# A fused transformer block on one core: the linear-attention factor products by k in two halves, and three fp32 row sums as pairs of rounded matmuls

## The chip, the core and the metric

The kernel runs on one core of one Trainium2 chip. The metric is the device time of one execution in microseconds. Before the change it is 561.61 us, the median of 3 runs (560.68 to 561.68).

## What is computed

The reference, cut to what matters here (S = 2048 tokens, D = 512, 32 heads of 16):

```python
mod = silu(c) @ w_mod                       # six vectors: sa, ca, ga, sb, cb, gb
h = layernorm(x) * (1 + ca) + sa
q, k, v = split(h @ wqkv)                   # 32 heads of 16
phi = lambda t: where(t > 0, t + 1, exp(t)) + 1e-6
kv  = einsum("bhsd,bhse->bhde", phi(k), v)
z   = sum over s of phi(k)
o   = (phi(q) @ kv) / (phi(q) . z + 1e-6)
x = x + ga * (o @ wo)
h = layernorm(x) * (1 + cb) + sb
x = x + gb * (((h @ w_gate) * (h @ w_up)) @ w_down)
```

All tensors are fp32.

## The kernel before

**Number format.** A fp32 operand is held as a pair of tiles: a high part, rounded to the matmul's rounded fp32 format by a ScalarE copy, and a low part, the difference, taken by VectorE. `split` (L192) makes such a pair, `split_raw` (L196) with fresh buffers, and `product` (L202) multiplies two lists of pairs with three matmuls a pair: high by high (L206), high by low (L207), low by high (L208). A plain fp32 matmul needs no pair.

**Stages.** Tokens come in 16 tiles of 128 (4 chunks of 4). The first stage makes the k side: for each tile the normalized rows times the k weights, phi, and `t_tile` (L350), which accumulates x-hat transposed times phi(k) in four PSUM banks `tacc`. So v is never formed for each token: at the end `tacc` is scaled by ca and gets zb x sa added, which gives four factors of 128 rows (k = 0 to 3, L736 to L743), and these times the v weights give kv. Beside it, `z_add` (L336) sums phi(k) over the tiles in `zacc`. The main loop (L612) runs over tiles 4 to 15. In each iteration i the matmuls of a later projection stand first, then the elementwise work, then `t_tile(i)`, then what the table `extra` (L552) holds for i: splits of the v weights (4 to 7), the modulation sums `mod_part` of further vectors (8 to 14), the split of the wo weights (14), and the row sums.

**Row sums.** `mod_row` (L184) sums a 128 x 512 tile over its partitions and spreads the result to all partitions with one fp32 matmul by a 128 x 128 tile of ones (L186). It does so for ga (i = 11) and gb (i = 15). The same is done for `zacc` in the last iteration (L654), whose result `zb` (L656) everything in the next stage needs.

**The stage between.** L731 to L771 is an order written out by hand. `den_z`, `den_p`, `den_r`, `den_a`, `den_b` make the denominators: `den_p` (L676) is phi(q) times zb, on GpSimd unless `on` names VectorE; `den_r` (L682) the sum over each head; `den_b` (L691, L692) adds a constant and takes the reciprocal for a chunk; `den_c` (L711) multiplies phi(q) by it. `q_a` and `q_b` (L310, L311 on ScalarE; L314 on VectorE) make phi(q) from a projection's bank, and `q_b` frees that bank. The four factors are scaled on ScalarE (L738), completed on VectorE (L739), split (L193, L194), and multiplied with the v weights in 48 matmuls of 128 columns (L749), group g of 128 columns by group, with all k inside. The block-diagonal mask (L757) and a split give `kvp`; `w_out` (L719) multiplies it with the wo pairs, scales by ga (L725) and splits the result to `wp`. q projections 6 to 10 stand between these. Then tile by tile `turn_a` (four transposes of phi(q), L782), `turn_h` and `turn_l` (the split, L786 and L790) and `y_a` (12 matmuls with `wp`, L807) make the attention output; the second half of the kernel, from there on, is the gated block.

**What sets the order.** The program's order is each engine's order: nothing is rescheduled. Buffers come from pools: 99 SBUF tiles (`tiles`), and 4 + 4 PSUM banks (`ps_acc`, `ps_w`). `bank()` takes from `ps_w`, so a projection waits until the bank that it gets has been read.

Of the kernel before, what the change touches and what calls it, by code (L numbers as in the profile page):

```python
# [14 lines left out]
P = 128  # L15
# [7 lines left out]
def tile_adaln_block(  # L23
# [57 lines left out]
    def bank():  # L81
        return T(ps_w, "bank")
# [1 line left out]

    ident = consts.tile([P, P], F32, name="ident")
    make_identity(nc, ident)
    ones = consts.tile([P, P], F32, name="ones")
    nc.gpsimd.memset(ones, 1.0)
    mask = consts.tile([P, P], F32, name="mask")
    nc.gpsimd.memset(mask, 1.0)  # L90
    m3 = mask.rearrange("p (b i) -> p b i", i=DH)
# [67 lines left out]
    def silu():  # L159
        nc.scalar.activation(ce, ct, AF.Exp, scale=-1.0)  # L160
        nc.vector.tensor_scalar(ce, ce, 1.0, None, op0=ALU.add)
        nc.vector.reciprocal(ce, ce)
        nc.vector.tensor_mul(sc, ct, ce)
# [9 lines left out]
    def mod_col(acc, ps):  # L173

        for b in range(KD):
            nc.tensor.matmul(ps[:, b:b + 1], acc[:, b * P:(b + 1) * P], ones[:, 0:1], start=True, stop=True)
        return ps

    def col_out(v, ps, add):
# [1 line left out]
        nc.vector.tensor_scalar(t, ps[:, :KD], add, None, op0=ALU.add)  # L181
        return t

    def mod_row(v, acc):  # L184
        ps = bank()
        nc.tensor.matmul(ps, ones, acc, start=True, stop=True)  # L186
        t = consts.tile([P, D], F32, name=f"row{v}")
        nc.scalar.activation(t, ps, AF.Copy)
        return t
# [9 lines left out]
        split(raw, h[:raw.shape[0]], l[:raw.shape[0]], low)  # L199
        return h, l  # L200

    def product(ps, pairs):  # L202

        n = len(pairs)
        for i, ((ah, al), (bh, bl)) in enumerate(pairs):
            nc.tensor.matmul(ps, ah, bh, start=i == 0, stop=False)  # L206
            nc.tensor.matmul(ps, ah, bl, start=False, stop=False)  # L207
            nc.tensor.matmul(ps, al, bh, start=False, stop=i == n - 1)  # L208

    def product2(pss, pairs):  # L210

# [152 lines left out]
    def q_b(i):  # L364
        phi_b(q_ps.pop(i), phq[i])
# [16 lines left out]
    def sums_in(b):  # L382
        return ps_idle if b == 1 else ps_m
# [12 lines left out]

    def block_one(v, b):
        at = at_of(v, b)
        nc.tensor.matmul(sums_in(b)[:, at:at + 1], sums[v, b // 2][:, b % 2 * P:(b % 2 + 1) * P], ones[:, 0:1],
                         start=True, stop=True)  # L400

    def block_out(b):
# [38 lines left out]

    keep_on(18)
    n0.stats(0)
    silu()
    n0.stats(1)
    n0.rstd_of(0, 2)
# [97 lines left out]
    def mod_load(*vs):  # L544
        raw_m.update({v: load_mod(v) for v in vs})

    def mod_part(v, *ks):
        if 0 in ks:
            accs[v] = B("f")
        mod_acc(accs[v], raw_m[v], ks)  # L550
# [4 lines left out]
             7: lambda: (wv.extend(split_raw(r) for r in raw_v[3:4]),),  # L555
             8: lambda: (mod_part(2, 0, 1), mod_load(3)),
             9: lambda: (mod_part(2, 2, 3), mod_load(4)),
             10: lambda: (mod_part(3, 0, 1, 2), mod_load(5)),
             11: lambda: (mod_part(3, 3), mod_part(4, 0, 1), rows.update({2: mod_row(2, accs[2])})),
             12: lambda: (raw_o.extend(load(wo_v[k], "raw") for k in range(KD)), mod_part(4, 2, 3), cols.update({3: col_out(3, mod_col(accs[3], bank()), 0.0)})),  # L560
             13: lambda: (mod_part(5, 0, 1, 2), cols.update({4: col_out(4, mod_col(accs[4], bank()), 1.0)})),
             14: lambda: (mod_part(5, 3), wo_s.extend(split_raw(x) for x in raw_o)), 15: lambda: rows.update({5: mod_row(5, accs[5])})}
    q_at = {4: 3}
    ahead = {}

# [46 lines left out]
    for i in range(4, NT):  # L612
# [31 lines left out]
            q_b(q_at[i])  # L644
        if i + 1 < NT:
            z_add(i + 1)
        if ch + 2 < NCH and j == 2:
            nx2.nmr_of()
            nx2.xhat(0, 1)
        if ch + 2 < NCH and j == 3:  # L650
            nx.xhat(3)
        if i == NT - 1:
            zps = bank()
            nc.tensor.matmul(zps, ones, zacc, start=True, stop=True)  # L654
# [78 lines left out]
    den_a(0, 0, 1, on=nc.vector)  # L733
    ps = proj(6, wq)
    fs, tt = [], []
    for k in range(KD):  # L736
        f = B("n")
        nc.scalar.activation(f, tacc[k], AF.Copy, scale=ca[:, k:k + 1])  # L738
        nc.vector.scalar_tensor_tensor(f, zb, sa[:, k:k + 1], f, op0=ALU.mult, op1=ALU.add)  # L739
# [536 lines left out]
```

## Time and profile before

| | |
|---|---|
| median of 3 runs | 561.61 us |
| profiled execution | 561.47 us |
| span in its profile | 559.8 us |
| TensorE clock granted | 1.00 |
| TensorE busy, matmuls | 551.9 us, 2544 instructions |
| VectorE busy | 379.8 us, 648 instructions |
| ScalarE busy | 294.2 us, 531 instructions |
| GpSimd busy | 207.4 us, 226 instructions |

The profile calls TensorE PE (its weight loads PEld), VectorE DVE, ScalarE ACT, GpSimd POOL, and the DMA-issuing engine SP. A row of a timeline gives the start and the duration in microseconds, the engine, the source line, the operation, output and input tiles by name, the shape, and how many instructions were merged; in brackets stands the idle time before it and what ended it. Matmul durations are modelled and overlap, so that consecutive starts tell more than durations.

### The profile page before, as it was taken

How to read it: one execution, taken by the hardware profiler on the slowest of the kernel's cores; microseconds unless marked ns; L12 is line 12 of the kernel's file. 1: busy time of each engine (PE TensorE's matmuls, PEld its weight loads, DVE VectorE, ACT ScalarE, POOL GpSimd, SP SyncE). 2: the span in 40 equal slices, each digit the busy share in tenths (PEclk: the TensorE clock that was granted, in tenths of full speed). 3: DMA queues.
4: the chain of work that ended last, by engine and by line, in shares of the span. 5: the costliest groups of instructions: out<-in, count | busy, mean ns of one | idle time of the engine just before them, and what ended most of it. 6: DMA issues, size and time to landing. Idle time of an engine off the chain costs nothing.

```text
span 559.8 us, 7391 instructions
## 1 busy us (share of the span) xinstructions
PE 551.9 (99%) x2544; PEld 453.5 (81%) x2544; DVE 379.8 (68%) x648; ACT 294.2 (53%) x531; POOL 207.4 (37%) x226
## 2 busy tenths in 40 slices
PE   7999999999999999999999999999999999999997
PEld 5888888888888888888888888878888888888775
DVE  5968779869898998865655766862455545444653
ACT  3876858446476877663545355553444334334420
POOL 2000000003327646343556644485424455554200
PEclk9999999999999999999999999999999999999999
DMA  8910224202230020151446136598353211200004
GB/s 254 384 39 1 75 76 150 77 0 71 80 114 2 0 76 0 39 159 68 150 151 195 32 122 221 178 363 286 114 157 87 57 39 48 71 0 1 0 1 150
DMA packets 50133, 57.24 MB, mean 102 GB/s; under 512 B 6384, under 2 KB 28912, under 8 KB 50096
## 3 DMA queue, kind: packets, MB, share of 16 engines
q1 hardware_dynamic: 50096, 56.77, 31.8%
q8 instruction: 20, 0.33, 0.3%
q14 instruction: 17, 0.14, 0.1%
HBM read 43.12 MB, written 13.63 MB: 101 GB/s over the span
## 4 chain that ended last, share of the span: by engine, by line
PE 94%; DVE 3%; DMA 1%; SPq 0%; issue 0%; ACT 0%; POOL 0%
PE bank L970 38%; PE acc L807 8%; PE acc L1048 7%; PE acc L1049 7%; PE acc L1050 7%; PE bank L206 5%; PE bank L207 5%; PE bank L208 5%; PE acc L357 2%; PE acc L355 2%; PE acc L356 2%; PE bank L271 2%; PE acc L439 1%; DMA x<-in_A_x_dram 1%; PE bank L782 1%; PE acc L271 1%
## 5 line engine op out<-in xcount | busy, mean ns | idle before, releaser
L970 PE MATMUL bank<-h,w 128*128 128x512 f32 (+1 forms) x924 | 215.8, 390 | 0.0
L970 PEld LDWEIGHTS bank<-h,w 128*128 128x128 f32 (+1 forms) x924 | 170.8, 185 | 38.6 <-issue 0.4
L976 ACT ACTIVATE bank<-bank 128x512 f32<-128x512 f32 (+1 forms) x44 | 25.6, 581 | 151.2 <-PE bank L970 151.1
L956 POOL TENSOR_TENSOR w<-raw,w 128x256 fp32r<-128x256 f32 (+3 forms) x44 | 46.1, 1048 | 157.2 <-ACT w L949 150.0
L996 DVE TENSOR_TENSOR phi<-bank,g 128x512 f32<-128x512 f32 (+1 forms) x22 | 15.1, 688 | 83.5 <-PE bank L970 79.8
L1048 PE MATMUL acc<-w,kh 128*128 128x512 f32 (+1 forms) x176 | 68.6, 390 | 0.0
L1049 PE MATMUL acc<-w,kh 128*128 128x512 f32 (+1 forms) x176 | 68.6, 390 | 0.0
L1050 PE MATMUL acc<-w,kl 128*128 128x512 f32 (+1 forms) x176 | 68.5, 389 | 0.0
L956 POOL TENSOR_TENSOR w<-t,w 128x512 fp32r<-128x512 f32 (+1 forms) x44 | 57.4, 1305 | 0.0
L1055 DVE TENSOR_TENSOR x<-acc,x 128x512 f32<-128x512 f32 x80 | 50.3, 681 | 8.6 <-PE acc L1050 8.6
L206 PE MATMUL bank<-w,h 128*128 128x512 f32 x112 | 44.8, 400 | 0.0
L208 PE MATMUL bank<-w,h 128*128 128x512 f32 x112 | 43.7, 390 | 0.0
L207 PE MATMUL bank<-w,h 128*128 128x512 f32 x112 | 43.6, 390 | 0.0
L676 POOL TENSOR_TENSOR f<-h,zb 128x512 f32<-128x512 f32 x12 | 17.1, 1439 | 67.8 <-ACT zb L656 49.2
L249 POOL TENSOR_TENSOR rstd<-ve,half 128x4 f32<-128x4 f32 (+3 forms) x12 | 11.2, 930 | 83.0 <-DVE ve L246 71.4
L807 PE MATMUL acc<-w,xh 128*128 128x512 f32 x128 | 40.7, 399 | 0.0
L1048 PEld LDWEIGHTS acc<-w,kh 128*128 128x128 f32 (+1 forms) x176 | 33.0, 188 | 7.1
L1050 PEld LDWEIGHTS acc<-w,kl 128*128 128x128 f32 (+1 forms) x176 | 33.0, 188 | 7.0
L1049 PEld LDWEIGHTS acc<-w,kh 128*128 128x128 f32 (+1 forms) x176 | 33.1, 188 | 6.9
L938 POOL TENSOR_TENSOR t<-raw,t 128x256 f32<-128x256 f32 (+1 forms) x44 | 36.9, 838 | 1.7
L1022 DVE TENSOR_TENSOR g<-bank,u 128x512 f32<-128x512 f32 (+1 forms) x22 | 15.2, 691 | 27.0 <-ACT u L976 27.0
L264 ACT ACTIVATE n<-x,nmr,rstd 128x512 f32<-128x512 f32 x31 | 23.7, 808 | 14.6 <-DVE nmr L254 14.4
(159 smaller groups left out, 1011.3 us busy)
## 6 DMA issues: line engine op xcount, KB each, us to landing
x<-in_A_x_dram SPq DMA_DIRECT2D x24, 256.0 KB, 5.2
raw<-in_w_mod_dram SPq DMA_DIRECT2D x24, 256.0 KB, 3.8
raw<-in_B_w_gate_dram SPq DMA_DIRECT2D x40, 128.0 KB, 3.0
raw<-in_B_w_up_dram SPq DMA_DIRECT2D x40, 128.0 KB, 3.1
raw<-in_B_w_down_dram SPq DMA_DIRECT2D x20, 256.0 KB, 3.1
side_s<-h SPq DMA_DIRECT2D x16, 256.0 KB, 2.5
h<-side_s SPq DMA_DIRECT2D x16, 256.0 KB, 5.5
out_dram<-x SPq DMA_DIRECT2D x16, 256.0 KB, 2.6
```

Source lines behind the costliest of these rows:

```text
L206: nc.tensor.matmul(ps, ah, bh, start=i == 0, stop=False)
L207: nc.tensor.matmul(ps, ah, bl, start=False, stop=False)
L208: nc.tensor.matmul(ps, al, bh, start=False, stop=i == n - 1)
L807: nc.tensor.matmul(yps[i], x, y, start=fresh and k + n == 0, stop=k == KD - 1 and n == 2, skip_group_check=True)
L938: sub = lambda out, x, y: (on or nc.gpsimd).tensor_tensor(out, x, y, op=ALU.subtract)
L956: sub = lambda out, x, y: (on or nc.gpsimd).tensor_tensor(out, x, f32(y), op=ALU.subtract)
L970: mm = lambda x, y, **kw: nc.tensor.matmul(ps, x[:, k], y, skip_group_check=True, **kw)
L976: nc.scalar.activation(out, x, AF.Copy)
L1048: nc.tensor.matmul(dn[j], hh[:n, a:b], dh[:n], start=i == 0, stop=False)
L1049: nc.tensor.matmul(dn[j], hh[:n, a:b], dl[:n], start=False, stop=False)
L1050: nc.tensor.matmul(dn[j], hl[:n, a:b], dh[:n], start=False, stop=i == n_of - 1)
L1055: nc.vector.tensor_tensor(xt, dn[j], xt, op=ALU.add)
```

## The change

Four things are edited.

1. The three row sums (ga, gb, zacc) take a pair, high and low, and two matmuls with a rounded tile of ones. `ones` shrinks to one column; `ones_r` is cast from it on VectorE in the prologue. The pairs are made in iterations 10, 13 and (zacc) 14. To make room, one `mod_part` of vector 5 moves from 13 to 12, one from 14 to 13, and the first wo split from 14 to 13.
2. The factors and their splits no longer stand as two loops: after the four scalings comes factor, high, and the low of the factor before, in turn.
3. The 48 products of 128 columns are ordered by k outside and g inside, k = 0, 1 before q projection 8 and k = 2, 3 after it, in a bank of `ps_acc` in place of `ps_w`. The denominators of tiles 2 and 3 (`den_a`) stand ahead of the mask.
4. What follows moves: q projection 9 stands whole between kv and `w_out(0, 1)`, `den_b` behind `q_b(8)` and not in front of it, q projection 10 between the two `w_out`, `den_c(1)` behind `turn_h(0)`, and q projection 11 in two halves around the transposes of tile 0.

```diff
-    ones = consts.tile([P, P], F32, name="ones")
+    ones = consts.tile([P, 1], F32, name="ones")
     nc.gpsimd.memset(ones, 1.0)
+    ones_r = consts.tile([P, P], F32R, name="ones_r")
...
-    def mod_row(v, acc):
+    def over_rows(ps, pair):
+        for m, x in enumerate(pair):
+            nc.tensor.matmul(ps, ones_r, x, start=m == 0, stop=m == 1)
+
+    def mod_row(v, pair):
         ps = bank()
-        nc.tensor.matmul(ps, ones, acc, start=True, stop=True)
+        over_rows(ps, pair)
...
-    def product(ps, pairs):
+    def product(ps, pairs, begin=True, end=True):
...
     n0.stats(0)
+    nc.vector.tensor_copy(ones_r, ones.to_broadcast([P, P]))
     silu()
...
-             10: lambda: (mod_part(3, 0, 1, 2), mod_load(5)),
+             10: lambda: (accs.update({2: split_raw(accs[2])}), mod_part(3, 0, 1, 2), mod_load(5)),
...
-             12: lambda: (raw_o.extend(load(wo_v[k], "raw") for k in range(KD)), mod_part(4, 2, 3), cols.update({3: col_out(3, mod_col(accs[3], bank()), 0.0)})),
-             13: lambda: (mod_part(5, 0, 1, 2), cols.update({4: col_out(4, mod_col(accs[4], bank()), 1.0)})),
-             14: lambda: (mod_part(5, 3), wo_s.extend(split_raw(x) for x in raw_o)), 15: lambda: rows.update({5: mod_row(5, accs[5])})}
+             12: lambda: (raw_o.extend(load(wo_v[k], "raw") for k in range(KD)), mod_part(4, 2, 3), mod_part(5, 0), cols.update({3: col_out(3, mod_col(accs[3], bank()), 0.0)})),
+             13: lambda: (mod_part(5, 1, 2, 3), wo_s.extend(split_raw(x) for x in raw_o[:1]), accs.update({5: split_raw(accs[5])}), cols.update({4: col_out(4, mod_col(accs[4], bank()), 1.0)})),
+             14: lambda: (wo_s.extend(split_raw(x) for x in raw_o[1:]),), 15: lambda: rows.update({5: mod_row(5, accs[5])})}
...
             z_add(i + 1)
+        if i + 1 == NT - 1:
+            zpair = split_raw(zacc)
...
-            nc.tensor.matmul(zps, ones, zacc, start=True, stop=True)
+            over_rows(zps, zpair)
...
+    def tt_high(k):
+        f = fs[k]
+        nc.vector.scalar_tensor_tensor(f, zb, sa[:, k:k + 1], f, op0=ALU.mult, op1=ALU.add)
+        tt.append((B("w", dt=F32R), B("w", dt=F32R)))
+        nc.scalar.activation(tt[k][0], f, AF.Copy)
+
+    def tt_low(k):
+        nc.vector.tensor_tensor(tt[k][1], fs[k], f32(tt[k][0]), op=ALU.subtract)
+
+    def kv_part(*ks):
+        for k in ks:
+            for g in range(KD):
+                a, b = g * P, (g + 1) * P
+                (ah, al), (bh, bl) = cut(wv[k], a, b), cut(tt[k], a, b)
+                for n, (x, y) in enumerate(((ah, bh), (ah, bl), (al, bh))):
+                    nc.tensor.matmul(kvps[:, a:b], x, y, start=k + g + n == 0, stop=k == KD - 1 and n == 2,
+                                     skip_group_check=True)
+
     for k in range(KD):
-        f = B("n")
-        nc.scalar.activation(f, tacc[k], AF.Copy, scale=ca[:, k:k + 1])
-        nc.vector.scalar_tensor_tensor(f, zb, sa[:, k:k + 1], f, op0=ALU.mult, op1=ALU.add)
-        fs.append(f)
-    for f in fs:
-        tt.append((B("w", dt=F32R), B("w", dt=F32R)))
-        split(f, *tt[-1])
+        fs.append(B("n"))
+        nc.scalar.activation(fs[k], tacc[k], AF.Copy, scale=ca[:, k:k + 1])
+    for k in range(KD):
+        tt_high(k)
+        if k:
+            tt_low(k - 1)
+    tt_low(KD - 1)
     q_a(6, ps)
     q_tile(7)
-    kvps = bank()
-    for g in range(KD):
-        a, b = g * P, (g + 1) * P
-        product(kvps[:, a:b], [(cut(wv[k], a, b), cut(tt[k], a, b)) for k in range(KD)])
+    kvps = acc_bank()
+    kv_part(0, 1)
     q_b(6)
     q_b(7)
     den_p(1, 2)
-    den_a(0, 2, on=nc.vector)
     ps = proj(8, wq)
+    den_a(0, 2, 3, on=nc.vector)
+    kv_part(2, 3)
...
-    den_p(0, 3, on=nc.vector)
     split(kvf, *kvp)
-    den_r(0, 3)
-    den_b(0)
     q_a(8, ps)
     ps = proj(9, wq)
     q_b(8)
+    den_b(0)
+    q_a(9, ps)
     w_out(0, 1)
-    q_a(9, ps)
-    den_c(0, 1)
+    q_b(9)
+    ps = proj(10, wq)
+    den_c(0)
+    q_a(10, ps)
     w_out(2, 3)
-    q_b(9)
-    q_tile(10)
+    ps = bank()
+    pairs = [(cut(norm[2].t[k], 3 * P, 4 * P), wq[k]) for k in range(KD)]
+    product(ps, pairs[:2], end=False)
...
     turn_a(0)
-    ps = proj(11, wq)
+    product(ps, pairs[2:], begin=False)
     turn_h(0)
+    den_c(1)
     turn_l(0)
```

More of the change, by code (lines that the diff above doesn't have):

```diff
@@ L175, in mod_col @@
         for b in range(KD):
-            nc.tensor.matmul(ps[:, b:b + 1], acc[:, b * P:(b + 1) * P], ones[:, 0:1], start=True, stop=True)
+            nc.tensor.matmul(ps[:, b:b + 1], acc[:, b * P:(b + 1) * P], ones, start=True, stop=True)
         return ps
@@ L200, in split_raw @@
         return h, l
-    def product(ps, pairs):
+    def product(ps, pairs, begin=True, end=True):
         n = len(pairs)
         for i, ((ah, al), (bh, bl)) in enumerate(pairs):
-            nc.tensor.matmul(ps, ah, bh, start=i == 0, stop=False)
+            nc.tensor.matmul(ps, ah, bh, start=begin and i == 0, stop=False)
             nc.tensor.matmul(ps, ah, bl, start=False, stop=False)
-            nc.tensor.matmul(ps, al, bh, start=False, stop=i == n - 1)
+            nc.tensor.matmul(ps, al, bh, start=False, stop=end and i == n - 1)
     def product2(pss, pairs):
@@ L398, in block_one @@
         at = at_of(v, b)
-        nc.tensor.matmul(sums_in(b)[:, at:at + 1], sums[v, b // 2][:, b % 2 * P:(b % 2 + 1) * P], ones[:, 0:1],
+        nc.tensor.matmul(sums_in(b)[:, at:at + 1], sums[v, b // 2][:, b % 2 * P:(b % 2 + 1) * P], ones,
                          start=True, stop=True)
```

## Prediction

> **What bounds the kernel now.** I began with the busy shares and the chain of work that ended last.
>
> ```profile
> PE 551.9 (99%) x2544; PEld 453.5 (81%) x2544; DVE 379.8 (68%) x648; ACT 294.2 (53%) x531; POOL 207.4 (37%) x226
> ...
> PE 94%; DVE 3%; DMA 1%; SPq 0%; issue 0%; ACT 0%; POOL 0%
> ```
>
> TensorE is busy for 551.9 of 559.8 us and 94% of the chain is its work. So a microsecond leaves the time only if TensorE loses work, or one of its few waits. A wait added on VectorE counts only when a matmul stands behind it. The second view is the list of waits between 126 and 160 us, the stretch that the change rewrites: total, times, longest.
>
> ```profile
> PEld bank L207 <- DVE w L194: 0.4, 2, 0.2
> PEld bank L782 <- DVE n L725: 0.3, 1, 0.3
> ```
>
> Both are TensorE's weight loads waiting for VectorE: twice in the 128-column products for a low of L194, once in the first transposes (L782) for a bank that the last multiply of L725 still reads. The sizes come from TensorE's timeline, whose rows give start and duration. The durations of matmuls overlap, so I price by the distance between starts.
>
> **The pace, and the three row sums.**
>
> ```profile
> 103.82 1.02 PE L186 MATMUL bank<-f,ones 128*128 128x512 f32 x2
> ...
> 107.44 0.39 PE L355 MATMUL acc<-kh,xh 128*128 128x512 f32 x1
> ...
> 125.67 1.02 PE L654 MATMUL bank<-z,ones 128*128 128x512 f32 x2
> ...
> 129.30 1.02 PE L186 MATMUL bank<-f,ones 128*128 128x512 f32 x2
> ...
> 132.92 0.39 PE L206 MATMUL bank<-w,h 128*128 128x512 f32 x1
> ...
> 135.42 0.39 PE L208 MATMUL bank<-w,h 128*128 128x512 f32 x1
> ```
>
> The last two rows are 11 rounded matmuls of 512 columns apart: 2.50 / 11 = 0.227 us each. Between each row sum's start and the matmul that follows its 12 successors lie 107.44 - 103.82 = 3.62, 129.30 - 125.67 = 3.63 and 132.92 - 129.30 = 3.62 us. Less 12 x 0.227 = 2.72, one fp32 row sum costs 0.90 (the trace shows it as two passes). Its replacement, two rounded matmuls, costs 2 x 0.227 = 0.45. **Removed: 3 x 0.45 = 1.35 us.** No rounded matmul with ones as the stationary operand is in this trace; its bounds are 0.227 and the 0.45 of an fp32 pass, and I take 0.227, since width and number format are those of the row.
>
> The cover of what this adds: each row sum needs a high (ScalarE) and a low (VectorE) of its sum. For accs[2] and accs[5] the matmul comes an iteration or more later. The tight one is zacc.
>
> ```profile
> 122.33 0.68 DVE L340 TENSOR_TENSOR z<-z,phi 128x512 f32<-128x512 f32 x1
> 122.93 0.74 DVE L171 SCALAR_TENSOR_TENSOR f<-raw,sc,f 128x512 f32<-128x512 f32 x1
> 123.59 2.49 DVE L194 TENSOR_TENSOR w<-raw,w 128x512 fp32r<-128x512 f32 x4
> 127.16 0.69 DVE L314 SCALAR_TENSOR_TENSOR h<-bank,h 128x512 f32<-128x512 f32 x1 [1.08 <-ACT h L311]
> ```
>
> zacc is whole at 123.0; a copy and a low of some 0.65 each end at 124.3, before the row sum at 125.67: 1.4 us of margin. One of the four w lows and the mod_part work go into the iteration before, so L194 still ends near 126.1, ahead of the 1.08 us of idle time in front of L314. I cost this at nothing; without that cover it would be some 0.7. The new copy ones_r is cast in the prologue:
>
> ```profile
> 5.11 0.16 DVE L163 TENSOR_TENSOR sc<-ct,ce 128x4 f32<-128x4 f32 x1
> 6.08 0.69 DVE L237 BATCH_NORM_STATS2 st<-x 128x6 f32<-128x512 f32 x1 [0.81 <-DMA x<-in_A_x_dram]
> ```
>
> The trace has no 128x128 cast; the 128x128 add (L691, quoted below) takes 0.29. VectorE idles 0.81 there for the next x tile: free.
>
> **The v products by k.**
>
> ```profile
> 135.64 0.22 PE L206 MATMUL bank<-w,w 128*128 128x128 f32 x1
> ...
> 137.52 0.28 PE L206 MATMUL bank<-w,w 128*128 128x128 f32 x1
> ...
> 141.54 0.45 PE L206 MATMUL bank<-w,h 128*128 128x512 f32 x1
> 141.83 0.40 PE L207 MATMUL bank<-w,h 128*128 128x512 f32 x1
> ```
>
> From 137.52 to 141.54 run 36 products of 128 columns: 0.1117 each. The 48 take 141.83 - 0.23 - 135.64 = 5.96 us, of which 48 x 0.1117 = 5.36 is work. **0.60 us is waiting.** It goes if the lows come in time, which VectorE and ScalarE decide:
>
> ```profile
> 130.85 2.41 ACT L738 ACTIVATE n<-acc,both 128x512 f32<-128x512 f32 x4
> ...
> 132.05 2.73 DVE L739 SCALAR_TENSOR_TENSOR n<-zb,both,n 128x512 f32<-128x512 f32 x4
> 134.70 2.49 DVE L194 TENSOR_TENSOR w<-n,w 128x512 fp32r<-128x512 f32 x4
> 137.11 1.36 DVE L314 SCALAR_TENSOR_TENSOR h<-bank,h 128x512 f32<-128x512 f32 x2
> ```
>
> After the change TensorE reaches these products 1.35 earlier, at 134.29. VectorE's run into them starts at L314 (127.16), behind a q product that only the first row sum precedes, so it moves by 0.45 alone and L739 starts at 131.60. In the new order (factor, factor, low 0, factor, low 1, factor, low 2, low 3, each some 0.65) low 0 ends at 133.6 and low 1 at 134.9. The first half needs them at 134.4 and, 13 products in, at 135.74: margins of 0.8. Low 3 ends at 131.60 + 2.73 + 2.49 = 136.8, and the second half, after q product 8, starts at 134.29 + 24 x 0.1117 + 2.72 = 139.7. The 0.60 goes.
>
> **The first transposes.**
>
> ```profile
> 152.26 0.39 PE L208 MATMUL bank<-w,h 128*128 128x512 f32 x1
> 152.55 0.66 PE L782 MATMUL bank<-ident,h 128*128 128x128 f32 x4
> 153.15 0.50 PE L206 MATMUL bank<-w,h 128*128 128x512 f32 x1
> 153.48 0.39 PE L207 MATMUL bank<-w,h 128*128 128x512 f32 x1
> ...
> 156.01 0.60 PE L782 MATMUL bank<-ident,h 128*128 128x128 f32 x4
> ...
> 159.22 0.60 PE L782 MATMUL bank<-ident,h 128*128 128x128 f32 x4
> ```
>
> The second set of four, with 12 matmuls behind it, spans 159.22 - 156.01 = 3.21; less 2.72, four transposes cost 0.49. The first set spans 153.48 - 0.23 - 152.49 = 0.76: 0.27 is its wait. Now it stands behind both w_out pairs and half of q product 11, so this wait goes too. Together 1.35 + 0.60 + 0.27 = **2.2 us saved**. Everything else on TensorE keeps its count.
>
> **What the new order makes late.** The same TensorE work at its pace puts kv's second half at its end at 142.37, w_out(0) at 145.09, q product 10 at 146.45, w_out(2) at 149.17, q product 11 at 150.53, transposes 0 at 151.89, transposes 1 at 153.74 (before: 156.01). VectorE must follow.
>
> ```profile
> 138.38 1.32 DVE L676 TENSOR_TENSOR f<-h,zb 128x512 f32<-128x512 f32 x1
> 139.74 0.69 DVE L682 TENSOR_REDUCE den<-f 128x32 f32<-128x512 f32 x1
> ...
> 143.52 1.22 DVE L194 TENSOR_TENSOR xl<-n,xh 128x512 fp32r<-128x512 f32 x1
> 144.66 0.67 DVE L682 TENSOR_REDUCE den<-f 128x32 f32<-128x512 f32 x1
> 145.37 0.29 DVE L691 TENSOR_TENSOR den<-den,den 128x128 f32<-128x128 f32 x1
> 145.70 0.95 DVE L692 RECIPROCAL den<-den 128x128 f32<-128x128 f32 x1
> ...
> 147.93 1.37 DVE L725 TENSOR_TENSOR n<-bank,row 128x512 f32<-128x512 f32 x2 [0.74 <-PE bank L208]
> 149.32 1.38 DVE L194 TENSOR_TENSOR w<-n,w 128x512 fp32r<-128x512 f32 x2
> 150.61 1.29 DVE L711 SCALAR_TENSOR_TENSOR h<-h,den 128x512 f32<-128x512 f32 x2
> ...
> 137.87 2.97 POOL L676 TENSOR_TENSOR f<-h,zb 128x512 f32<-128x512 f32 x2 [7.01 <-DVE h L314]
> ```
>
> L676 and L194 take 0.68 alone (2.49 for four) but 1.32 and 1.22 while GpSimd runs its own L676; each has both ends in what follows. ScalarE's highs now wait for the factors in turn, so the last ends at 136.1, four activations of some 0.6 for q 6 and 7 end at 138.5, and q_b(7) at 139.2. Two den products and two reductions, now both ahead of the mask, end at 141.9 to 143.2. The mask waits for kv, 142.6, so it ends at 143.3 to 143.9, the high at 143.9 to 144.5, the low at 144.6 to 145.8; w_out needs the low at its third matmul, 145.54. q_b(8) frees the bank for q product 10 at 145.8 to 146.5 (needed 146.45). Then L691 and L692 (now ahead of w_out's multiplies, 1.2), L725 (1.37), L194 (1.38) and q_b(9): 150.3 to 151.0, needed by q product 11 at 150.53, its bank. Then den_c(0), two multiplies, two lows and den_c(1), 3.8 in all: 154.1 to 154.8, needed by transposes 1 at 153.74. **Late by 0.35 to 1.1**, and it is one lateness seen at successive points, not a sum. I take 0.45, near the uncollided end, because GpSimd's two long instructions there fall beside ScalarE's and PSUM-fed work. The gain is 2.2 - 0.45 = 1.75, and from y 0 on the order is the old one, so it stays to the end.
>
> A rule of the Trainium skill speaks against this change here: the page SBUF — State Buffer, section Who interferes with whom, says that a VectorE instruction with two SBUF inputs and a GpSimd instruction that reads SBUF exclude each other, the loser blocking for the whole instruction. The rows 1.32 and 1.22 against 0.68 agree with it. By the rule each further collision would cost up to one GpSimd instruction, and the time would come out as in the second rival.
>
> **The rivals.** *All waits hidden*: VectorE comes 0.45 earlier than I walked it; 2.2 saved, 559.4. For it: only the last of five points is surely late; against it: den_c(1) stands behind four lows. *VectorE becomes the bound*: the upper ends hold (late 1.1) and one more low collides (0.6): 2.2 - 1.7 = 0.5 saved, 561.1; with the upper ends alone 560.5. For it: at the upper ends four of the five points come late. Against it: before the change VectorE had 0.74 and other idle pieces here. *The row sums keep their price* (0.45 per rounded matmul): 1.75 - 1.35 = 0.4 saved, 561.2. Against it: every rounded row of this width paces 0.227. *Slower*: the place is the same stretch of VectorE; four lows of w_out and two den_c can each lose 0.6 to GpSimd, 3.6 on top of 1.1, 4.7 late: 2.5 lost, 564.1. The gain is gone from 2.2 late, so from two of the six collisions on top of the upper ends; slower than 0.2% needs four. Against it: GpSimd has only two den products left there, and each blocks one VectorE instruction at a time.
>
> **How the numbers follow.** The profiled execution took 561.47 (span 559.8 and 1.7 around it), 0.14 under the median of 561.61. Its sum gives 561.47 - 1.75 = 559.7; against the median 561.61 - 1.75 = 559.86, and I say 559.8. Chances: forecast (gain 1.4 to 2.1) 0.50; all hidden 0.15; VectorE the bound 0.28, of which 0.11 above 1.1 us of gain; row sums 0.04; slower 0.03. 0.2% is 1.1 us, about what a measurement can tell from no change. Faster 0.50 + 0.15 + 0.11 = 0.76; same 0.17 + 0.04 = 0.21; slower 0.03. The range from 558.9 (all hidden, and the 0.5 by which runs of one kernel differ) to 561.0 (gain 0.6) leaves about 0.2 out.
>
> **What would show it.** In the changed kernel's timeline: the row sums' spacing 3.17 for 3.62; no VectorE wait in the 128-column products, each half 2.7 long; transposes 0 without a wait; transposes 1 waiting for L719 (the changed file's den_c) by about 0.4. Wrong would be: a wait of w_out(0) or of q products 10 and 11 over 0.3 us, L194 at 1.2 in the w_out lows, or a lost microsecond after y 0.

## The result, and the profile after

The changed kernel takes 559.94 us (median of 22 runs, 558.13 to 562.77). Before, measured beside it, takes 562.28 (22 runs, 560.37 to 564.58): a ratio of 0.9961 with a 95% interval of 0.9948 to 0.9974, so 1.5 to 2.9 us saved, 2.2 in the middle. The prediction said 559.8 within 558.9 to 561.0.

All the edits stand between the first row sum and the first y product, but for two small pieces of edit 1 ahead of it: the cast of `ones_r` in the prologue and the pair of ga's sum in iteration 10. I call what lies between the stretch and measure it in each trace, from the start of the first matmul of ga's row sum to the start of the first matmul that writes y 0. What varies before and after it does not enter: 52.54 us in the profile before, 50.58 in the profile after. TensorE's timeline of the changed kernel in it (start, duration):

```profile
103.66 0.62 PE L187 MATMUL bank<-w,ones_r 128*128 128x512 f32 x2
...
106.83 0.39 PE L360 MATMUL acc<-kh,xh 128*128 128x512 f32 x1
...
125.06 0.62 PE L187 MATMUL bank<-w,ones_r 128*128 128x512 f32 x2
...
128.23 0.61 PE L187 MATMUL bank<-w,ones_r 128*128 128x512 f32 x2
...
131.41 0.39 PE L211 MATMUL bank<-w,h 128*128 128x512 f32 x1
...
134.13 2.79 PE L760 MATMUL acc<-w,w 128*128 128x128 f32 x24
136.75 0.45 PE L211 MATMUL bank<-w,h 128*128 128x512 f32 x1
...
139.59 2.79 PE L760 MATMUL acc<-w,w 128*128 128x128 f32 x24
142.22 0.45 PE L211 MATMUL bank<-w,h 128*128 128x512 f32 x1
...
151.85 0.60 PE L810 MATMUL bank<-ident,h 128*128 128x128 f32 x4
152.21 0.48 PE L211 MATMUL bank<-w,h 128*128 128x512 f32 x1
...
153.45 0.40 PE L213 MATMUL bank<-w,h 128*128 128x512 f32 x1
153.83 0.66 PE L810 MATMUL bank<-ident,h 128*128 128x128 f32 x4
154.24 0.70 PE L835 MATMUL acc<-w,xh 128*128 128x512 f32 x2
```

A row sum now has two matmuls (L187, x2), and from one to the matmul behind its 12 successors lie 106.83 - 103.66 = 3.17, 128.23 - 125.06 = 3.17 and 131.41 - 128.23 = 3.18 us, where 3.62 stood before. Each half of the v products is one merged row of 24 and takes 136.75 - 134.13 = 2.62 and 142.22 - 139.59 = 2.63; no wait splits it. The first transposes follow their matmul at once. Only the second ones come late: 153.83 - 153.45 = 0.38 after the last matmul, 0.15 over the pace of 0.227. The waits of TensorE's weight loads between 126 and 160 us (total, times, longest) name it:

```profile
PEld bank L810 <- DVE h L719: 0.4, 1, 0.4
```

Outside the stretch the two profiles do not agree so well. The profiled execution after took 561.02 (span 559.3), only 0.45 below its counterpart before, because 1.7 us were lost again near 375 us. The waits of the changed kernel's weight loads from 370 to 382 us:

```profile
PEld bank L998 <- DMA h<-side_s: 1.9, 5, 0.5
```

There the next stage reads rows back from memory, and TensorE waits for these loads five times. The code at this place is the old one. Whether the change shifts the loads into a collision or one execution merely had bad luck is a question for a second profile.

### The profile page after: what moved, and what is told of

It reads as the page before. It is cut to its first block, busy times and chain, and to the rows that moved or that the text cites. A ratio compares the mean times of both kernels' runs of the same rounds, so it can differ in the third digit from the quotient of the medians.

```text
span 559.3 us, 7392 instructions
## 1 busy us (share of the span) xinstructions
PE 552.5 (99%) x2544; PEld 454.1 (81%) x2544; DVE 380.5 (68%) x652; ACT 296.2 (53%) x534; POOL 208.2 (37%) x226
## 4 chain that ended last, share of the span: by engine, by line
PE 89%; DMA 4%; DVE 2%; SPq 2%; ACT 1%; issue 1%; POOL 0%; POOLq 0%
PE bank L998 32%; PE acc L835 8%; PE acc L1076 7%; PE acc L1077 7%; PE acc L1078 6%; PE bank L211 5%; PE bank L213 5%; PE bank L212 5%; PE acc L362 3%; PE acc L360 3%; PE acc L361 3%; PE acc L444 2%; PE bank L276 2%; DMA h<-side_s 1%; DMA h<-side_a 1%; PE bank L810 1%
## 5 line engine op out<-in xcount | busy, mean ns | idle before, releaser
L998 PE MATMUL bank<-h,w 128*128 128x512 f32 (+1 forms) x924 | 217.1, 391 | 0.4 <-DMA h<-side_s 0.2
L998 PEld LDWEIGHTS bank<-h,w 128*128 128x128 f32 (+1 forms) x924 | 170.5, 185 | 40.6 <-DMA h<-side_s 1.9
L684 POOL TENSOR_TENSOR f<-h,zb 128x512 f32<-128x512 f32 x12 | 17.5, 1474 | 62.2 <-ACT zb L664 48.7
```

The lines of the kernel that those rows point to most:

```text
L998: mm = lambda x, y, **kw: nc.tensor.matmul(ps, x[:, k], y, skip_group_check=True, **kw)
```

## The experiments

The theory to be tested is the prediction's sum, with its three independent savings (row sums 1.35, waits in the v products 0.60, first transposes 0.27) less a lateness of VectorE. The rivals: that the savings hang on one another, that an edit is idle, and that the loss near 375 us belongs to the change. In the two kernels that were profiled twice the stretch repeats within 0.05 us; each variant has one profile. Against the times, about 1 us can be told.

### Both kernels again

No edit: the kernel before (e3), and the changed one (e4).

> The kernel before once more, for a second profile. Two questions on the profiled executions: does the prologue lose time to a granted clock below 1, and does TensorE wait for the loads of the side tiles near 372 to 378 us? If both differ between executions of one kernel (theory), the span differs by up to 2 to 3 us with an unchanged stretch of 52.5. Rival: this kernel never waits there, and the 1.7 us that the changed kernel's profile lost near 375 us is the change's own.

> The changed kernel once more. Theory: the stretch is 50.6 again, 1.9 to 2.0 less than before, the wait for the side tiles near 372 us is of another size or absent, and the ratio of times lies at 0.996. Rival (the change gives time back at the edge between the two sides): TensorE waits about 1.7 us near 375 again and the gain over the whole span is about 0.5.

Stretches of 52.53 (before) and 50.62 (after); times 562.27 and 560.68 (12 runs of after, 559.39 to 563.97; ratio 0.9968, 0.9948 to 0.9989). The gated block, from the start of its first matmul (L970, L998 changed) to the start of the last, is 345.88 in e4, 345.92 in e3 and 345.91 in the first profile of before; only the first profile of after has 347.59. TensorE, weight loads, VectorE, ScalarE, GpSimd, granted clock, DMA share and GB/s in two windows, first of the profile after, then of e4:

```profile
12.00:16.00 4.00, 3.75 (x18) 3.27 (x19) 3.39 (x10) 3.27 (x6) 0.00 (x0) 0.71 1.07 372
372.00:378.00 6.00, 5.59 (x21) 3.31 (x20) 4.96 (x7) 1.72 (x4) 3.90 (x5) 1.00 0.95 329
```

```profile
12.00:16.00 4.00, 3.44 (x24) 3.02 (x24) 3.32 (x10) 2.56 (x4) 0.00 (x0) 0.94 1.08 367
16.00:20.00 4.00, 4.00 (x13) 3.13 (x12) 3.89 (x8) 2.52 (x5) 0.00 (x0) 0.64 1.06 388
372.00:378.00 6.00, 6.00 (x28) 4.80 (x27) 5.20 (x8) 2.10 (x4) 5.23 (x6) 1.00 1.06 389
```

In e4 TensorE is busy throughout 372 to 378 and 389 GB/s move, for 329 in the execution that waited. So that loss is not the change's. The rows at 12 to 20 us show what else varies between executions of one program: the clock granted in the prologue (0.71, 0.94, 0.64). In the kernel before it was 1.00 there in the first profile, and in e3 0.63:

```profile
16.00:20.00 4.00, 4.00 (x14) 3.14 (x12) 3.61 (x8) 2.15 (x4) 0.00 (x0) 0.63 1.05 387
```

The fourteen profiles of all kernels, whose code up to the first row sum is nearly the same, show where the 4 us come from over which the runs of one kernel spread. That row sum starts at 102.84 and 103.82 us where the prologue's clock stayed at 1.00, at 103.66 to 105.51 in the ten where it was 0.50 for 3.41 us, and at 106.47 and 106.95 in the two where it was 0.50 for twice as long. From y 0 to the end it takes 403.31 to 403.45 us in all but two, the first profile after with 405.07 and that of e1 below with 404.42, and in both TensorE waits for these loads.

### The row sums alone

The changed row sums (edit 1) in the old order:

```diff
-    for k in range(KD):
-        tt_high(k)
-        if k:
-            tt_low(k - 1)
-    tt_low(KD - 1)
+    for k in range(KD):
+        f = B("n")
+        nc.scalar.activation(f, tacc[k], AF.Copy, scale=ca[:, k:k + 1])
+        nc.vector.scalar_tensor_tensor(f, zb, sa[:, k:k + 1], f, op0=ALU.mult, op1=ALU.add)
+        fs.append(f)
+    for f in fs:
+        tt.append((B("w", dt=F32R), B("w", dt=F32R)))
+        split(f, *tt[-1])
...
-    kvps = acc_bank()
-    kv_part(0, 1)
+    kvps = bank()
+    for g in range(KD):
+        a, b = g * P, (g + 1) * P
+        product(kvps[:, a:b], [(cut(wv[k], a, b), cut(tt[k], a, b)) for k in range(KD)])
...
```

> Edit 1 alone: three row sums as pairs of rounded matmuls, the stage between in its old order. Measure: the stretch from the start of the ga row sum to the first y product on TensorE, 52.54 us before (103.82 to 156.36) and 50.58 after the whole change. Theory (the gains need each other): TensorE comes 1.35 earlier to the v products, but VectorE's factors and lows only 0.45, since two of the row sums stand behind the q product that starts VectorE's run. So the wait inside the v products grows by some 0.9, and the stretch is about 52.1, a gain of 0.45. Rival (each gain stands alone): the full 1.35, a stretch of 51.2. In time about 0.1% against 0.25% faster.

Both missed in the time and the stretch: 565.76 us (12 runs, 559.83 to 567.63; before 562.82; ratio 1.003, 0.9998 to 1.0062), and a stretch of 56.98, 4.4 longer than before. TensorE's timeline, then windows with the clock in the column before the DMA share:

```profile
134.31 0.22 PE L211 MATMUL bank<-w,w 128*128 128x128 f32 x1
135.04 0.33 PE L212 MATMUL bank<-w,w 128*128 128x128 f32 x1 [0.51 <-DVE w L199]
...
135.32 0.27 PE L211 MATMUL bank<-w,w 128*128 128x128 f32 x1
135.64 0.33 PE L212 MATMUL bank<-w,w 128*128 128x128 f32 x1
...
139.16 0.41 PE L212 MATMUL bank<-w,w 128*128 128x128 f32 x1
139.37 0.41 PE L213 MATMUL bank<-w,w 128*128 128x128 f32 x1
```

```profile
136.00:137.00 1.00, 0.90 (x6) 0.61 (x6) 1.00 (x3) 0.97 (x3) 0.00 (x0) 1.00 0.97 252
137.00:138.00 1.00, 1.00 (x10) 1.00 (x11) 1.00 (x3) 0.34 (x1) 0.46 (x1) 0.96 0.83 208
...
141.00:142.00 1.00, 1.00 (x7) 1.00 (x6) 0.00 (x0) 0.00 (x0) 0.92 (x3) 0.50 0.00 0
...
147.00:148.00 1.00, 1.00 (x3) 0.72 (x3) 0.96 (x2) 0.00 (x0) 0.00 (x0) 0.50 0.65 225
148.00:149.00 1.00, 1.00 (x5) 0.83 (x4) 0.29 (x1) 0.02 (x1) 0.00 (x0) 0.92 0.66 188
```

TensorE reaches the v products 1.35 earlier, VectorE's lows end only 0.4 earlier (L199 starts at 134.30, L194 at 134.70 before): the first wait is 0.62 (135.04 - 134.31 - 0.11), three more of 0.21 follow, 1.26 us together. With the product behind each wait, which comes 0.05 late as well, this is 1.47 for the 0.60 of before, which holds such products too: 0.87 more, as the theory said. Then, from 137.9 to 148.2, the granted clock is 0.50 and a 128-column product takes 139.37 - 139.16 = 0.21 instead of 0.11. In the 12 runs the mean clock has two kinds: in six it is 0.987 or 0.988 (566.3 to 567.6 us), in three 1.000 (559.8 to 560.3; the five of before at 1.000 took 560.5 to 561.9), with three between. Half of the 10.24 us at 0.50 is 5.1: without the fall the stretch would be about 51.9 by this estimate, 0.7 less than before. No execution of before, nor of any other kernel told of so far, had a clock under 0.991.

### The order alone

Edits 2 to 4 with the old fp32 row sums: the two matmuls of `over_rows` become `nc.tensor.matmul(ps, ones, acc, start=True, stop=True)` again, without the pairs.

> Edits 2 to 4 alone, the row sums left as fp32 matmuls. Theory: the wait in the v products (0.60) and the one at the first transposes (0.27) go, and because TensorE is 1.35 later than in the changed kernel and VectorE only 0.45, nothing comes late behind them: a stretch of 51.67, a gain of 0.87, no wait of transposes 1. Rival (the order is what makes VectorE late, whatever TensorE does): transposes 1 wait as after the whole change, 0.2 to 0.4, and the gain is about 0.5.

561.71 us (559.66 to 564.42; ratio 0.9989, 0.9967 to 1.0012), stretch 51.93, a gain of 0.61. The clock is 1.00 throughout the stretch. The 0.27 of the first transposes did go, but den_c(1) came as late for the second ones as in the whole change (1.97 from first to second, 1.98 there). So the rival held: the order makes VectorE late there, also with row sums of the old length. With 1.35 for the row sums, 0.61 makes the measured 1.96: once the lows come in time, the two halves of the change add.

### The factors in two loops

Only edit 2 undone:

```diff
-    for k in range(KD):
-        tt_high(k)
-        if k:
-            tt_low(k - 1)
-    tt_low(KD - 1)
+    for k in range(KD):
+        nc.vector.scalar_tensor_tensor(fs[k], zb, sa[:, k:k + 1], fs[k], op0=ALU.mult, op1=ALU.add)
+    for f in fs:
+        tt.append((B("w", dt=F32R), B("w", dt=F32R)))
+        split(f, *tt[-1])
```

> The changed kernel with the four factors computed in one loop and their highs and lows in a second, as before; all else as changed. Theory: low 0 ends after four factors instead of one, at 134.9 on the clock of the prediction, where the second v product wants it at 134.4: one wait of 0.5 to 0.6 there and none later, since 12 products (1.34) lie between one low and the next. Stretch 50.6 + 0.4 to 0.6 = 51.0 to 51.2, the 0.15 that the second transposes waited for den being absorbed. Rival (later covers hide it, VectorE ends at the same time in either order): 50.6. On the clock: one wait of 0.6 is no more than what before lost there at full clock, so 1.00; if the clock falls with any wait at this place, the stretch grows by 4 to 5 us in most executions.

560.76 us (559.83 to 562.78; ratio 0.9973, 0.9956 to 0.9989), stretch 51.25, so 0.65 of the gain is lost; the theory's 51.0 to 51.2 is closest, though the second transposes wait as in the whole change (1.97 from the first), which it had as absorbed. The waits of TensorE's matmuls between 125 and 160 us have one row, and the clock stays 1.00:

```profile
PE acc L760 <- DVE w L199: 0.5, 1, 0.5
```

### The v products by output columns

The halves and the order by k undone, the lows in turn kept. First (e7) with `kv_part`'s loops exchanged (`for g` outside, `for k` inside, each block of columns with its own start) in the accumulator bank; then (e10) with before's own code:

```diff
-    kvps = acc_bank()
-    kv_part(0, 1)
+    kvps = bank()
+    for g in range(KD):
+        a, b = g * P, (g + 1) * P
+        product(kvps[:, a:b], [(cut(wv[k], a, b), cut(tt[k], a, b)) for k in range(KD)])
...
-    kv_part(2, 3)
```

> The changed kernel with the 48 v products in one go and by output columns (all four k of one block of 128 columns, then the next), as before; factors and lows stay in turn. Theory: the first block of columns needs low 1 after 4 products, low 2 after 7 and low 3 after 10 and meets them some 0.2, 0.9 and 0.3 late: 1.3 to 1.5 us of waiting in the first dozen products, stretch 52.0 to 52.2 at full clock. Rival (it is the halves and the places of the q products that count, not the order of k): under 0.5 of waiting, 50.6 to 51.1. On the clock: the waits are as many and as long as with the row sums alone (1.3 in 2.6 us), so if they bring the fall, the clock drops to 0.50 from about 138 to 148 us in most executions and the stretch is 56 to 57; if it does not fall here, something else in the row-sums-only kernel brought it.

> The changed kernel with before's own v products (by output columns, in one go, each block of columns with its own start, in a bank of the rotating four instead of a bank of the accumulators) and lows in turn. At full clock: waits of 1.2 to 1.4 in the first dozen products, stretch 51.8 to 52.2. Theory of the clock (several waits among the first 128-column products, over 1.2 us together within 3 us, bring it to 0.50 for some 10 us): about half of the executions or more have a granted clock of 0.988 or less and take 566 to 569, the others 560 to 562.5; a profile with the fall has a stretch of 56 to 57. Rival (something in the kernel of the run before, its accumulator bank, brought it there): no execution below 0.990.

The kernel of e7 does not compute what the reference does, so only its times are read. It alone starts four blocks of columns one by one in a bank of the accumulators, which `y_seed` later fills from ScalarE and `y_a` adds to without a start; whether that is the reason, no run here tests. Its times are 564.13 (559.92 to 569.01), with a clock of 0.984 to 0.988 in five of ten runs, and its profile has the fall and a stretch of 56.97. e10: 566.38 (560.83 to 569.00; ratio 1.0043, 1.001 to 1.0076), with a clock of 0.984 to 0.988 in 7 of 12 runs, 566.4 to 569.0, and 0.994 or more in the others, 560.8 to 563.5. Its profile is of an execution without the fall, stretch 52.13, and shows the bare price of the waits:

```profile
135.56 0.27 PE L211 MATMUL bank<-w,w 128*128 128x128 f32 x1
136.06 0.33 PE L212 MATMUL bank<-w,w 128*128 128x128 f32 x1 [0.23 <-DVE w L752]
...
136.33 0.28 PE L211 MATMUL bank<-w,w 128*128 128x128 f32 x1
137.32 0.33 PE L212 MATMUL bank<-w,w 128*128 128x128 f32 x1 [0.71 <-DVE w L752]
```

The waits for the lows of k = 1, 2 and 3 are 0.39, 0.88 and 0.40 over the pace, 1.67 together. So the order by k, not the place of the q products, takes the wait away, and the accumulator bank is not what brings the clock down.

### All v products in one go

`kv_part(0, 1, 2, 3)` ahead of q product 8, the second call gone.

> The changed kernel with all 48 v products by k in one go ahead of q product 8; all else as changed. Theory (the order by k and the lows in turn take the wait away, the split into halves does nothing): low 3 is ready at 136.8 and wanted after 36 products at 138.3, so no wait; the stretch is that of the change, 50.5 to 50.7. Rival (the second half behind q product 8 is needed, for the lows or for the bank that q product 8 takes): a wait of 0.3 or more at the fourth k or at q product 8 or 9, stretch 50.9 or more.

560.98 us (558.97 to 562.36; ratio 0.9968, 0.9945 to 0.999), stretch 50.53 with no wait but the one for L719, as the theory has it. The split into halves earns nothing here: with it the two profiles have 50.58 and 50.62.

### The old order behind the v products

Edit 4 undone: with the halves (e5), and with one go (e9). Behind the v products stands, in both, what stood there before (`den_a` of tile 3 and the places of q product 11 and den_c(1), not shown, go back too):

```diff
-    split(kvf, *kvp)
-    q_a(8, ps)
-    ps = proj(9, wq)
-    q_b(8)
-    den_b(0)
-    q_a(9, ps)
-    w_out(0, 1)
-    q_b(9)
-    ps = proj(10, wq)
-    den_c(0)
-    q_a(10, ps)
-    w_out(2, 3)
+    den_p(0, 3, on=nc.vector)
+    split(kvf, *kvp)
+    den_r(0, 3)
+    den_b(0)
+    q_a(8, ps)
+    ps = proj(9, wq)
+    q_b(8)
+    w_out(0, 1)
+    q_a(9, ps)
+    den_c(0, 1)
+    w_out(2, 3)
+    q_b(9)
+    q_tile(10)
```

> The changed kernel with the order behind the v products put back: rounded row sums, factors and lows in turn and the two halves by k stay; the mask, den, w_out, q products 9 to 11 and the first transposes stand as before. Theory (the row sums give 1.35, the waits in the v products 0.60, the new tail almost nothing): the stretch from the first row sum to the first y product, 52.54 before and 50.6 after, comes out at 50.6 to 50.9, with the wait of the first transposes (0.27 before) still there and no wait for den at the second. Rival (the tail's new order is what lets VectorE follow): with the old one w_out or the transposes wait 0.6 to 1.2 longer, stretch 51.2 to 51.8. On the clock, where the row sums alone had it fall to 0.50 for 10 us: if the waits between the 128-column products bring that, the clock is 1.00 from 134 to 150 us here and no execution has the clock of 0.987; if the shorter row sums bring it, most executions still take 564 to 567.

> Rounded row sums and factors in turn as changed, the 48 v products by k in one go ahead of q product 8, and behind them the old order of everything: two q products (8 and 9) then lie between the v products' end and w_out, as before the change; where the halves had the old order behind them, only q product 9 did, and w_out(1) waited 1.2 for its bank. Theory (the halves cost q product 8 its place as cover, and the new order behind them only pays that back): row sums 1.35 and waits 0.6 come through, stretch 50.6 to 50.8, and w_out waits for nothing. Rival (the old order keeps VectorE too late in any case, since its idle 1.31 before the mask is used up when TensorE comes 1.95 earlier and VectorE 0.45): w_out or its multiplies wait 0.5 to 1.2, stretch 51.2 to 52.0.

Here my theory fell twice, and the rival held, though its sizes did not: 51.2 to 51.8 for e5, and for e9 a wait of 0.5 to 1.2 at w_out. e5: 561.71 us (559.71 to 564.27; ratio 0.9985, 0.9962 to 1.0009), stretch 52.15, so 1.57 of the 1.96 is gone. e9: 561.03 (560.13 to 563.47; ratio 0.9973, 0.9955 to 0.999), stretch 51.22, 0.69 over one go with the new order. TensorE's timeline of e5, then of e9:

```profile
146.87 0.39 PE L213 MATMUL bank<-w,xl 128*128 128x512 f32 x1
148.27 0.50 PE L211 MATMUL bank<-w,xh 128*128 128x512 f32 x1 [1.01 <-DVE h L319]
```

```profile
146.63 0.39 PE L213 MATMUL bank<-w,xl 128*128 128x512 f32 x1
147.16 0.50 PE L211 MATMUL bank<-w,xh 128*128 128x512 f32 x1
...
151.14 0.39 PE L213 MATMUL bank<-w,h 128*128 128x512 f32 x1
151.58 0.65 PE L807 MATMUL bank<-ident,h 128*128 128x128 f32 x4
```

w_out(1) waits for the bank that q_b(8) (L319) frees, 1.17 over the pace with the halves (148.27 - 146.87 - 0.23), 0.30 in one go, and the first transposes wait 0.2 again. VectorE has den_p, den_r and den_b between the mask and q_b(8). With the halves only q product 9 lies between the v products' end and w_out, and no longer 8 and 9. But also with both there the old order is late. So the new order behind the v products is worth 0.7 by itself and 1.6 once the halves are there. In e5 TensorE stood still for 1.17 us between matmuls of 512 columns, and the clock stayed 1.00 from 146 to 150.

### One long wait

To see what in the waits brings the clock down, one wait alone, by three reductions whose results nobody uses, ahead of the factors:

```diff
+    idle = consts.tile([P, 1], F32, name="idle")
+    for k in range(3):
+        nc.vector.tensor_reduce(idle, zb, axis=AX.X, op=ALU.add)
     for k in range(KD):
         tt_high(k)
```

> The changed kernel with three reductions of zb over its 512 columns (0.6 each, their result unused) on VectorE ahead of the factors: low 0 ends 1.8 later, about 135.35 on the changed kernel's profile, where the second v product wants it at 134.24: one wait of 1.1, and none behind it, since the lows come every 1.27 and 12 products take 1.34. At full clock the stretch is 50.6 + 0.9 to 1.1 = 51.5 to 51.7. First theory of the clock (the sum of the waiting counts, over about 1 us in 3): the clock falls to 0.50 behind the wait as with the row sums alone, in half of the executions or more, and those take 565 to 568. Second theory (it takes several waits with few 128-column products between them; one wait of 1.2 in the 512-column products of w_out left the clock at 1.00): no execution below 0.990, all within 559 to 564.

564.50 us (560.57 to 566.79; ratio 1.0022, 0.9998 to 1.0045). The clock is under 0.991 in 3 of 12 runs, 565.6 to 566.8, with two at 0.991, and one such run is the profiled one, stretch 55.31:

```profile
136.83 0.33 PE L760 MATMUL acc<-w,w 128*128 128x128 f32 x1 [0.54 <-ACT w L749]
137.55 2.83 PE L760 MATMUL acc<-w,w 128*128 128x128 f32 x18 [0.40 <-DVE w L752]
```

```profile
138.00:138.50 0.50, 0.50 (x6) 0.50 (x6) 0.50 (x2) 0.30 (x1) 0.00 (x0) 1.00 0.96 246
...
139.00:140.00 1.00, 1.00 (x7) 1.00 (x6) 1.00 (x2) 0.54 (x2) 0.00 (x0) 0.50 1.00 294
...
144.00:144.50 0.50, 0.50 (x3) 0.40 (x2) 0.50 (x1) 0.00 (x0) 0.50 (x1) 0.50 0.00 0
```

The high came late too, so there are two waits with one product between them, 0.70 and 0.61 over the pace, and none later: the single wait was not reached. The fall comes at 139.0 and lasts to 145.8. Waits scattered over the first dozen products, as the second theory had them, are not needed; that one wait alone would do, this run does not show. The first theory holds with a weaker share, 3 to 5 of 12 where I said half.

### den_c(1) ahead of the lows

The one wait that is left, taken away, on top of one go: `w_out(2, 3, mid=lambda: den_c(1))`, where `mid` is called between the multiplies and the lows, and the later `den_c(1)` gone.

> The changed kernel with the v products by k in one go and den_c(1) ahead of the lows of w_out(2) and w_out(3). Theory: the second transposes no longer wait for L719 (0.15); the two lows end 0.6 later at 153.8, before y 0 wants them at 154.6 or later; stretch 50.35 to 50.45 against 50.53 in one go and 50.6 as changed; in the time this is 0.2 us, less than the spread of the executions. Rival (turn_l(0), now straight behind those lows, or the lows themselves come late for y 0): a wait of 0.2 or more in y 0, stretch 50.6 to 50.9.

559.99 us (7 runs, 558.83 to 561.53; ratio 0.995, 0.9929 to 0.9972), stretch 50.79. The second transposes no longer wait: 1.83 after the first ones, for 1.98 as changed. But in this profile the 48 products took 5.61 instead of 5.31 in e8, since low 0 was late, and q product 11 came 0.1 late behind q_b(9). VectorE's row tells why:

```profile
127.62 1.85 DVE L684 TENSOR_TENSOR f<-h,zb 128x512 f32<-128x512 f32 x1
```

GpSimd ran two L684 of its own from 126.36 to 128.92, and VectorE's took 1.85, ending 0.55 after GpSimd's second, for the 0.68 that it takes alone. The two that VectorE runs there took 1.85 and 0.68, where in the profile after they took 0.68 and 1.09. The Trainium skill's page SBUF — State Buffer, section Who interferes with whom, has this rule (the loser blocks for the whole instruction), and the trace agrees. So 0.15 was gained and 0.3 lost to this collision, which none of the other thirteen profiles has at that place. Part of the rival is there too: in y 0, behind the stretch, the first matmul that reads the transposed low costs 0.07 more. The interval overlaps that of the change repeated (0.9948 to 0.9989), so none of the variants is shown to beat it.

## Why the prediction was right, step by step

- **The row sums, 1.35.** Right to a hundredth: 3.17 for 3.62, and two matmuls with ones as the stationary operand go at 0.227 each. The pairs cost nothing that the stretch shows: zacc's low ended 1.16 ahead of its row sum, where the prediction had 1.4. In the prologue, which varies by 4 us, a cast of 0.19 could not be seen.
- **The waits in the v products, 0.60.** Right, for the reason given: lows 0 and 1 ended 0.58 and 0.66 ahead of the products that read them, where the walk had 0.8. Without the lows in turn 0.65 comes back (e6), without the order by k 1.60 (e10 against e8): more than 0.60, since the earlier row sums lengthen the waits (1.47 in e1). The prediction did walk TensorE 1.35 and VectorE 0.45 earlier, and its sum holds for the full change. What it did not say is that the first two terms do not add by themselves: the row sums alone lengthen the waits, and in six of twelve executions the clock fell (e1).
- **The first transposes, 0.27.** Right: no wait at L810's first row.
- **VectorE late by 0.35 to 1.1, taken 0.45.** The place was right (L719 for the second transposes), the size was not: 0.15. This is the term that was mis-sized. The walk put den_c(1)'s end at 154.1 to 154.8, and it ended at 153.8 (153.9 on the clock of before, whose first row sum starts 0.16 later). The rows of VectorE after:

```profile
139.13 0.93 DVE L684 TENSOR_TENSOR f<-h,zb 128x512 f32<-128x512 f32 x1
...
149.29 0.68 DVE L319 SCALAR_TENSOR_TENSOR h<-bank,h 128x512 f32<-128x512 f32 x1
...
151.88 1.29 DVE L199 TENSOR_TENSOR w<-n,w 128x512 fp32r<-128x512 f32 x2
153.09 0.68 DVE L719 SCALAR_TENSOR_TENSOR h<-h,den 128x512 f32<-128x512 f32 x1
```

  The den products took 0.93 and 1.06, between the ends 0.68 and 1.32, and the w_out lows 1.29 for two, as without a collision. q_b(9) ended at 150.0 (150.1 on the clock of before), for 150.3 to 151.0. The rule of the Trainium skill's page SBUF — State Buffer, section Who interferes with whom, is seen at work in the den products, but at a place where nothing waits. The walk also misread a row: the 1.22 of L194 in the profile before stood beside GpSimd's L938 (143.01 to 144.19), not beside its L676. So GpSimd had more left there than the two den products that the rival *Slower* counted. After the change kv's low at that place took 0.69, and GpSimd's instruction of 143.82 took 1.27 where its like took 0.74. e2 has the same wait with the old row sums, so the lateness belongs to the order.
- **What was left out of the sum.** Each group of 24 products is 0.06 faster than 24 x 0.1117, and the q product behind it 0.12 slower than 2.72 (136.75 to 139.59 is 2.84). There is one such pair more now: 0.06 lost. The second transposes to y 0 takes 0.41 for 0.35. So 2.22 - 0.15 - 0.06 - 0.06 = 1.95, and 1.96 was measured, between the forecast (1.75) and the rival in which all waits are hidden (2.2).
- **The landing on 559.94.** It is partly luck. The gain came out 0.2 larger in the stretch; the kernel before came out at 562.28 where the runs shown gave 561.61.
- **The rivals.** VectorE did not become the bound, the row sums did not keep their price, and nothing came out slower. But the prediction's slower rival had the wrong mechanism: what does get slower is a kernel that waits over a microsecond at the v products, where the clock halves in some executions (seen in the profiles of e1, e7 and e11, and in the mean clocks of e10), and not one with six collisions. No row of before showed a clock under 1.00 and the prediction weighed none.

Open: by what measure the gate tells a window that makes the clock fall (the last section has the one that fits these profiles), and why e7 computes something else.

## What to carry to other kernels

Before a faster piece of TensorE work is counted as saved, look at who feeds the next piece: here three row sums worth 1.35 us gained some 0.7 at best, and lost 3 us in the median, until the lows behind them were made earlier. When one operand is needed in parts, let the products follow the order in which the parts come, and give each reordering its own look at the engine that frees the banks. Measure a stretch between two fixed events of the trace when the whole time spreads by more than the change.

## What the runs showed of the hardware

- **The granted clock can halve on little waiting.** After 1.26 to 1.67 us of waiting within some 3 us among 128-column products the clock went to 0.50 in some executions. A wait of 0.6 (e6), or 1.17 among 512-column matmuls (e5), did not do it. The Trainium skill, page TensorE: Matmul & The Clock Gate, Part 1: The HAM clock gate, says that a gate halves the clock after an idle window of about 3.4 us and gives it back after about as long of sustained work, and that the window runs free of the kernel. The traces fit the window and its freedom. The low clock lasted 10.24 us in e1 and e7 and 6.83 in e11, and each time it came 119.47 us after the prologue's low clock had ended: 3, 3, 2 and 35 times 3.41. They do not fit the rest: no window here was idle, and in e1 TensorE was busy without a break from 138 to 148 at 0.50.
- **What sorts these windows is how many columns the matmuls streamed.** I lay each profile's grid of 3.41 us through its changes of clock and count, window by window, the columns of the matmuls that start in it. At 0.227 us for 512 a full window has 7680. The three falls followed windows of 2432 (e1, from 134.51), 1792 (e7) and 2816 columns (e11). The clock stayed low after 2048 to 2816, and came back after 3840 (e7) and 4096 (e1, e11). In the eleven profiles without a fall the emptiest window of the stretch had 3200 (e10), and 3328 or more in the others. Busy time does not sort them; here are e11's window and then e10's, with the clock before the DMA share:

```profile
135.56:138.97 3.41, 2.47 (x18) 1.87 (x16) 3.38 (x6) 1.89 (x3) 0.00 (x0) 1.00 0.70 173
```

```profile
134.17:137.58 3.41, 2.47 (x15) 1.99 (x14) 3.32 (x6) 2.02 (x4) 0.00 (x0) 1.00 0.57 136
```

  e10's window still held 1.1 us of 512-column matmuls, and its last wait fell into the next one. So whether an execution falls can hang on where the grid lies, which would explain how one kernel can do both. A 128-column product takes 0.112 where a quarter of a 512-column one is 0.057, so such a series streams half of what 512-column matmuls do even without a wait. No run here sets the grid or the columns on purpose: this is what the fourteen profiles have in common. In the first 18 us, with other kinds of matmul, the count does not sort the windows (1416 columns in one of before without a fall, 2828 in one of e3 with one).
- **The prologue's clock varies from one execution to the next**, in the kernel before as in the changed one: 0.63 to 1.00 in 16 to 20 us. So do the loads at 375 to 380 us: TensorE loses 1.7 us to them in one of the changed kernel's two profiles and 1.0 in e1, and nothing in the other twelve.
